# A written order for the start of a gated-mix kernel (FNet spectral branch and SwiGLU branch)

## The chip, the cores and the metric

The kernel runs on one core of one Trainium2 chip. The metric is the device time of one execution in microseconds (us); before the change the median of three runs is 711.37 us (711.16 to 711.52). A core has a matrix engine (TensorE, PE in the profile, whose weight loads have a row of their own, PEld), a vector engine (VectorE, DVE), an activation engine (ScalarE, ACT), GpSimd (POOL) and SyncE (SP). Each works through its own list of instructions in order; semaphores tie them together. DMAs are issued from SP, ACT or POOL.

## The reference, cut to what matters

```python
g = sigmoid((x * gate_w).sum(-1, keepdims=True))            # x: 2048 x 512
a = dft_seq_re @ (x @ dft_hid_re.T) - dft_seq_im @ (x @ dft_hid_im.T)
h = silu(x @ w1) * (x @ w3)                                 # w1, w3: 512 x 1376
b = h @ w2                                                  # w2: 1376 x 512
out = g * a + (1 - g) * b
```

All of it is float32. The change touches only the beginning of the work on `h`.

## The kernel before, in words

**Precision.** TensorE takes float32r operands. Each float32 block X is split into a high part (ScalarE copies X into a float32r tile: `high`, L108) and a low part (VectorE subtracts the high part from X: `low`, L111). A product of two blocks is then three matmuls, high·high, high·low and low·high, each 128 x 128 by 128 x 512.

**Fewer products.** 2 x 2 blocks of operands are multiplied with a seven-product scheme (Winograd's form of Strassen's), so sums of blocks are formed on VectorE first: on the x side T1 to T4 from the raw blocks B11, B12, B21, B22 (`sum_xo`, L207, and `split_xo`), on the weight side four sums of one weight set (`sums_wb`, L248 to L251), whose split parts are the tile `wb`. The three raw weight parts are the tile `wa`; of the four raw parts of a set, in the order of its load, the third is A22 and the fourth, A21, is needed raw only by the first item.

**Items.** The gate and up products run over `ITEMS`, pairs of a column chunk c of the weights and a half g of the tokens; one item gives two 128 x 512 blocks of `h`. An item has seven products of six matmuls. They go into PSUM banks: X (bank n % 4) takes four of them in turn, Y (bank 4 + n % 2) one, Z (bank 6 + n % 2) two. X and Y are begun LOOK = 3 items ahead: `first1(n)` is the first X product and its copy to `s1`, `first2(n)` the Y product, the addition `s1 += Y` on VectorE (L293), which frees the Y bank, and `gate1(n)` the Silu of `s1`. `gate_up(n)` does the rest of item n and, between its own products, `first1(n + 3)` and `first2(n + 3)`. Two lists, `early` and `mid`, hang further work into an item: `early` after its second bank of work is begun, `mid` after the low part of the next `wb`.

**The first items.** Item 0 is computed without the seven-product scheme (`plain`, eight half products of six matmuls into the banks C00, C10, C01, C11), because its operands arrive first. Then come `first1`, `first2` and `gate1` of items 1, 2 and 3, with all sums and splits that they and item 1 need written between them. A pool of warm-up matmuls (`WARM` = 11, L398) runs on a zeroed bfloat16 tile while the first loads are under way.

**Order.** Up to L674 (the line that switches to the written order, just before the loop over `gate_up`) the order of each engine's instructions is chosen by the scheduler from the program's dependencies; from there on every engine's list is the program order. The loads of the start all go through the SP queue: a 128 KB piece of weight set 0, x block B11 (512 KB), the other 384 KB of weight set 0, B21, B12, weight set 1, B22, weight sets 2 and 3.

Of the kernel before, what the change touches and what calls it, by code (L numbers as in the profile page):

```python
# [21 lines left out]
NG = NST // 2  # L22
NC = (F + P - 1) // P
NP2 = (NC + 1) // 2
WARM = 11
LOOK = 3
K = 9
W2_AT = (9, 11, 13, 15)
# [4 lines left out]
def fnet_swiglu_gate_kernel(  # L33
# [46 lines left out]
    def bank(k, name):  # L80
        return psum.tile([P, 512], F32, tag=f"ps{k}", name=name)
# [17 lines left out]
    def parts(name):  # L99
        return take(ZO, [P, 2, 4, 256], F32R, name)  # L100
# [12 lines left out]
    def split(hi, lo, src):  # L113
        high(hi, src)
        low(hi, lo, src)
# [79 lines left out]
    def load_xo(g, k):  # L195

        if g not in XO:
            XO[g] = (xo1 if g else xo0).tile([P, 2, 7, 2, 512], F32R, tag="xo", name=f"xo{g}")
        ST[g, k] = wide(f"xs{g}_{k}")
        nc.sync.dma_start(ST[g, k], xt[g, XRAW.index(k)])  # L200

    OPS = ("B11", "B21", "B22", "T1", "T2", "T3", "T4")
    SUMS = {"T1": ("B12", "B11"), "T2": ("B22", "T1"), "T3": ("B22", "B12"), "T4": ("B21", "T2")}
# [1 line left out]
    def sum_xo(g, k, t):  # L205
        ST[g, k] = t
        nc.vector.tensor_sub(t, *(ST[g, v] for v in SUMS[k]))  # L207
# [5 lines left out]
    def split_xo(g, k):  # L213
        split(*xo_parts(g, k))
# [6 lines left out]
    def load_w(w, lo=0, hi=4):  # L221
        if lo == 0:
            WS[w] = f4_a.tile([P, 4, 256], F32, tag=f"f4_{4 + w % (LOOK + 1)}", name=f"ws{w}")
        nc.sync.dma_start(WS[w][:, lo:hi].rearrange("p a n -> p (a n)"),  # L224
                          w13[SETS[w], :, lo * 256 : hi * 256])

    def load_wb(w, spare=False):
# [5 lines left out]
    def wa_parts(w, lo, hi):  # L233
        return (*(flat(WA[w][:, h, lo:hi]) for h in range(2)), flat(WS[w][:, lo:hi]))

    def prep_wa(w, lo=0, hi=3):

        if lo == 0:
            WA[w] = wap.tile([P, 2, 3, 256], F32R, tag="wa", name=f"wa{w}")
        split(*wa_parts(w, lo, hi))  # L240

    WU = {}

    def sums_wb(w):

        r = WS.pop(w)
        u = WU[w] = wup.tile([P, 4, 256], F32, tag="wu", name=f"wu{w}")
        nc.vector.tensor_add(u[:, 0], r[:, 3], r[:, 2])  # L248
        nc.vector.tensor_sub(u[:, 1], u[:, 0], r[:, 0])
        nc.vector.tensor_sub(u[:, 2], r[:, 0], r[:, 3])  # L250
        nc.vector.tensor_sub(u[:, 3], r[:, 1], u[:, 1])  # L251

    def wb_parts(w):
        return flat(WB[w][:, 0]), flat(WB[w][:, 1]), flat(WU[w])
# [1 line left out]
    def high_wb(w):  # L256
        WB[w] = wbp.tile([P, 2, 4, 256], F32R, tag="wb", name=f"wb{w}")
        high(wb_parts(w)[0], wb_parts(w)[2])

    def low_wb(w):  # L260
        low(*wb_parts(w))
        if w < K:
            nc.gpsimd.dma_start(wbsp[w], WB[w].bitcast(F32))

    def prep_wb(w):
        sums_wb(w)
        high_wb(w)
        low_wb(w)

    def prod(ps, n, wi, xi, start, chain=False):  # L270
        w = WSET[n]
# [15 lines left out]

    def first2(n):

        y = bank(4 + n % 2, f"Y{n}")  # L290
        prod(y, n, 1, 1, True)
        s1 = G[n][1]
        nc.vector.tensor_add(s1, s1, y)  # L293
        put_score(n, 0, s1)
# [37 lines left out]
    def gate_up(n):  # L332
        last = NI - 1
        x, s1 = G.pop(n)
        z = bank(6 + n % 2, f"Z{n}")
        if n == last - 1:

            u2, g1 = (s1p.tile([P, 512], F32, tag="s1", name=f"{k}_{n}") for k in ("u2", "g1"))
        else:
            h = hp.tile([P, 1024], F32, tag="h", name=f"h{n}")  # L340
            u2, g1 = h[:, :512], h[:, 512:]
        u4 = u4p.tile([P, 512], F32, tag="u4", name=f"u4_{n}")
        nw = WSET[n + 1] if n < last else 0
        if nw in WB or nw == 0:
            nw = None
        elif back(nw):
            load_wb(nw)
            nw = None
        wa = WSET[n + LOOK + 1] if n + LOOK < last else 0
        if wa in WA or wa == 0:  # L350
            wa = None
        else:
            load_w(wa, 0, 3 if back(wa) else 4)

        prod(x, n, 4, 4, False, True)
        nc.scalar.activation(u2, x, AF.Copy)
        run(early, n)
        prod(z, n, 5, 5, True, True)
        nc.scalar.activation(u4, z, AF.Copy)
        if nw is not None:  # L360
            sums_wb(nw)
        if n + LOOK <= last:
            first1(n + LOOK)
        if nw is not None:
            high_wb(nw)
        prod(x, n, 3, 3, False, True)
        nc.vector.tensor_add(u4, u4, x)  # L367
        if nw is not None:
            low_wb(nw)
        run(mid, n)  # L370
        prod(z, n, 2, 6, False, True)
        nc.vector.tensor_add(u2, u2, z)
        nc.vector.tensor_mul(u2, s1, u2)  # L373
        store_h(n, 0, u2)
        if wa is not None:
            WA[wa] = wap.tile([P, 2, 3, 256], F32R, tag="wa", name=f"wa{wa}")
            parts_a = wa_parts(wa, 0, 3)
            high(parts_a[0], parts_a[2])
        if n + LOOK <= last:
            first2(n + LOOK)  # L380
        if wa is not None:
            low(*parts_a)
        prod(x, n, 6, 2, False, True)
        nc.scalar.activation(g1, x, AF.Silu)
        put_score(n, 1, x)
        if n + LOOK <= last:
            gate1(n + LOOK)
        nc.vector.tensor_mul(g1, g1, u4)
        store_h(n, 1, g1)
        run(at_end, n)  # L390

    load_w(0, 0, 1)
    load_xo(0, "B11")
    warm = s1p.tile([P, 1024], mybir.dt.bfloat16, tag="s1", name="warm")[:, :512]
    nc.vector.memset(warm, 0.0)
    wps = bank(7, "wps")
    for n in range(WARM):
        nc.tensor.matmul(wps, warm[:, :P], warm, start=True, stop=True)  # L398
    nc.scalar.activation(act0, warm[:, :24], AF.Silu)

    def plain(b12, a21):

        c = {}

        def half(i, j, w, x, start):
            if start:
                c[i, j] = bank((0, 4, 6, 7)[2 * i + j], f"C{i}{j}")
            for r in range(2):
                sl = slice(r * P, (r + 1) * P)
                mm3(c[i, j], w(0, sl), w(1, sl), x(r, 0), x(r, 1), start and r == 0,  # L410
                    not start and r == 1)

        def wa(k):
            return lambda h, sl: WA[0][:, h, k, sl]

        def xb(k):
            return lambda q, h: XO[0][:, h, k, q, :]

        w21 = lambda h, sl: a21[:, h, sl]
        x12 = lambda q, h: b12[:, h, q * 512 : (q + 1) * 512]  # L420
        s1 = s1p.tile([P, 512], F32, tag="s1", name="s1_0")
        g1 = u4p.tile([P, 512], F32, tag="u4", name="g1_0")
        h = hp.tile([P, 1024], F32, tag="h", name="h0")
        yield half(0, 0, wa(0), xb(0), True)
        yield half(1, 0, w21, xb(0), True)
        half(0, 0, wa(1), xb(1), False)
        nc.scalar.activation(s1, c[0, 0], AF.Silu)
        yield half(1, 0, wa(2), xb(1), False)
        nc.vector.tensor_mul(h[:, :512], s1, c[1, 0])
        store_h(0, 0, h[:, :512])  # L430
        half(0, 1, wa(0), x12, True)
        yield half(1, 1, w21, x12, True)
        half(0, 1, wa(1), xb(2), False)
        nc.scalar.activation(g1, c[0, 1], AF.Silu)
        half(1, 1, wa(2), xb(2), False)
        nc.vector.tensor_mul(h[:, 512:], g1, c[1, 1])
        yield store_h(0, 1, h[:, 512:])

    load_w(0, 1, 4)
    load_xo(0, "B21")  # L440
    load_xo(0, "B12")
    load_w(1)
    load_xo(0, "B22")
    load_w(2)
    load_w(3)

    zt = parts("b12"), parts("a21")
    b12, a21 = zt[0].rearrange("p h a n -> p h (a n)"), zt[1][:, :, 0]
    step = plain(b12, a21)
    prep_wa(0, 0, 1)  # L450
    for q in range(2):
        split(XO[0][:, 0, 0, q], XO[0][:, 1, 0, q], ST[0, "B11"][:, q * 512 : (q + 1) * 512])
    next(step)
    split(a21[:, 0], a21[:, 1], WS[0][:, 3])
    next(step)
    prep_wa(0, 1, 3)
    split_xo(0, "B21")
    next(step)
    split(b12[:, 0], b12[:, 1], ST[0, "B12"])
    next(step)  # L460
    split_xo(0, "B22")
    next(step)
    free(*zt)
    WS.pop(0)
    load_w(4)
    prep_wa(1)
    first1(1)
    first2(1)
    gate1(1)
    sum_xo(0, "T1", hp.tile([P, 1024], F32, tag="h", name="t1"))  # L470
    sum_xo(0, "T2", ST[0, "B11"])
    prep_wa(2)
    first1(2)
    first2(2)
    gate1(2)
    split_xo(0, "T2")
    prep_wb(1)
    sum_xo(0, "T3", ST[0, "B12"])
    split_xo(0, "T3")
    prep_wa(3)  # L480
    first1(3)
    first2(3)
    gate1(3)
    split_xo(0, "T1")
    prep_wa(4)
    sum_xo(0, "T4", ST[0, "B21"])
    split_xo(0, "T4")
    free(*(ST[0, b] for b in ("B11", "B21", "B12", "B22")))

    def do(work, n, f, *a):  # L490
        work.setdefault(n, []).append(lambda: f(*a))


    for k in ("B11", "B21", "B12", "B22"):
# [176 lines left out]
        sum_c(m + LEAD + 1)  # L671
        split_c(m + LEAD)

    ctx.enter_context(tc.manual_schedule())  # L674
    for n in range(1, NI):
        gate_up(n)
        if ITEMS[n] == (NC - 1, 0):
# [317 lines left out]
```

## Time and profile before

| What | Value |
|---|---|
| median of 3 runs | 711.37 us (711.16 to 711.52) |
| the profiled execution: its time | 710.88 us |
| the profiled execution: its span, first to last instruction | 709.1 us |
| PE busy | 703.9 us, 3089 matmuls |
| VectorE busy | 604.6 us, 733 instructions |
| ScalarE busy | 369.6 us, 478 instructions |
| DMA | 172.54 MB, mean 243 GB/s |

Times in the profile are counted from the span's start. A row of the timeline gives the start, the length, the engine, the line, the operation with its output and inputs, the count, and in brackets how long the engine stood idle before it and what released it. Tile names have their numbers left out, so that all PSUM tiles X1, X2, ... read X. A "xo" is a split x block, "xs_B" a raw one, "ws" raw weights, "wu" sums of weights.

### The profile page before, as it was taken

Reading aid. Unit: us, or ns where it says so; the run is one execution under the profiler, and the core shown is the slowest. Engines: PE = TensorE matmul, PEld = TensorE weight load, DVE = VectorE, ACT = ScalarE, POOL = GpSimd, SP = SyncE. Lnnn points to the kernel's source line nnn. Section 1 sums busy time; section 2 is a strip of 40 time slices with the busy share of each in tenths; the row PEclk is TensorE's granted clock in tenths of the full one; section 3 lists DMA queues with packets and bytes.
Section 4 is the critical chain, followed back from the end, with each engine's and each line's share of the span. In section 5 each row is a group of like instructions: output and inputs, shape, how many; then the busy total and the mean of one; then the engine's idle time right before and its main releaser. Section 6 shows DMA issues by size and latency. Waiting matters only on the chain.

```text
span 709.1 us, 8589 instructions
## 1 busy us (share of the span) xinstructions
PE 703.9 (99%) x3089; PEld 579.1 (82%) x3089; DVE 604.6 (85%) x733; ACT 369.6 (52%) x478; POOL 64.0 (9%) x118
## 2 busy tenths in 40 slices
PE   9999999999999999999999999999999999999997
PEld 6888888888888888888888888888888888888886
DVE  6979988787679999887999599969997896898985
ACT  6665555655446754454554553544455455455451
POOL 0011111121110000000110001100110000000000
PEclk9999999999999999999999999999999999999999
DMA  7575546589997556712596238814999971773932
GB/s 281 196 295 215 211 188 253 186 313 359 413 412 271 220 207 232 288 60 89 175 358 254 90 122 322 342 48 190 382 419 416 354 270 58 296 285 135 323 119 89
DMA packets 45403, 172.54 MB, mean 243 GB/s; under 512 B 5296, under 2 KB 5424, under 8 KB 41520
## 3 DMA queue, kind: packets, MB, share of 16 engines
q1 hardware_dynamic: 32464, 118.50, 45.2%
q0 software_dynamic: 12608, 52.97, 18.9%
q8 instruction: 24, 0.39, 0.2%
q10 hardware_dynamic: 288, 0.52, 0.2%
q14 instruction: 19, 0.16, 0.1%
HBM read 114.82 MB, written 57.16 MB: 243 GB/s over the span
## 4 chain that ended last, share of the span: by engine, by line
PE 99%; DMA 1%; DVE 0%; ACT 0%; SPq 0%; issue 0%
PE P L119 69%; PE X L119 16%; PE Z L119 8%; PE Y L119 4%; PE C L119 2%; DMA xs_B<-xt 1%; DVE xo L111 0%; DVE zc L788 0%; ACT xo L108 0%; SPq L224 0%
## 5 line engine op out<-in xcount | busy, mean ns | idle before, releaser
L119 PE MATMUL P<-zo,a 128*128 128x512 f32 x1344 | 305.5, 390 | 0.0
L119 PEld LDWEIGHTS P<-zo,a 128*128 128x128 f32 x1344 | 252.1, 188 | 53.2 <-DVE zo L111 1.2
L108 ACT ACTIVATE zo<-B 128x1024 fp32r<-128x1024 f32 (+1 forms) x182 | 189.3, 1045 | 184.5 <-PE P L119 93.2
L111 DVE TENSOR_TENSOR zo<-B,zo 128x1024 fp32r<-128x1024 f32 (+1 forms) x182 | 217.9, 1204 | 48.2 <-ACT zo L108 47.4
L119 PE MATMUL P<-zo,H 128*128 128x512 f32 x468 | 106.2, 389 | 0.0
L119 PEld LDWEIGHTS P<-zo,H 128*128 128x128 f32 x468 | 87.9, 188 | 18.2
L645 DVE TENSOR_TENSOR B<-B,B 128x1024 f32<-128x1024 f32 (+1 forms) x78 | 93.0, 1192 | 0.1
L119 PE MATMUL X<-xo,wb 128*128 128x512 f32 x378 | 92.7, 390 | 0.0
L119 PEld LDWEIGHTS X<-xo,wb 128*128 128x128 f32 x378 | 71.0, 188 | 14.7
L119 PE MATMUL P<-zo,Y 128*128 128x512 f32 x336 | 76.3, 390 | 0.0
L119 PEld LDWEIGHTS P<-zo,Y 128*128 128x128 f32 x336 | 63.1, 188 | 13.1
L322 POOL DMA_DIRECT2D hsp<-h x42 | 23.0, 547 | 126.5 <-DVE h L373 75.6
L119 PE MATMUL X<-xo,wa 128*128 128x512 f32 x126 | 32.3, 390 | 0.0
L119 PE MATMUL Z<-xo,wa 128*128 128x512 f32 x126 | 32.3, 391 | 0.0
L119 PE MATMUL Y<-xo,wa 128*128 128x512 f32 x126 | 32.1, 390 | 0.0
L119 PE MATMUL Z<-xo,wb 128*128 128x512 f32 x126 | 32.1, 390 | 0.0
L648 DVE TENSOR_TENSOR B<-B,B 128x1024 f32<-128x1024 f32 x26 | 31.7, 1219 | 0.0
L863 ACT ACTIVATE zu<-P 128x512 f32<-128x512 f32 x32 | 19.1, 598 | 20.4 <-PE P L119 20.3
L367 DVE TENSOR_TENSOR u<-u,X 128x512 f32<-128x512 f32 x21 | 14.4, 687 | 17.7 <-PE X L119 15.5
L119 PEld LDWEIGHTS Z<-xo,wa 128*128 128x128 f32 x126 | 23.6, 188 | 5.3 <-DVE xo L111 0.4
L119 PEld LDWEIGHTS Y<-xo,wa 128*128 128x128 f32 x126 | 23.7, 188 | 4.9
L119 PEld LDWEIGHTS X<-xo,wa 128*128 128x128 f32 x126 | 23.7, 188 | 4.9
(134 smaller groups left out, 551.3 us busy)
## 6 DMA issues: line engine op xcount, KB each, us to landing
B<-cc SPq DMA_DIRECT2D x64, 512.0 KB, 6.1
hsp<-h POOLq DMA_DIRECT2D x42, 256.0 KB, 3.6
B<-hsp SPq DMA_DIRECT2D x20, 512.0 KB, 9.9
wbsp<-wb POOLq DMA_DIRECT2D x8, 1024.0 KB, 4.3
wb<-wbsp SPq DMA_DIRECT2D x8, 1024.0 KB, 7.8
B<-zsp SPq DMA_DIRECT2D x16, 512.0 KB, 8.4
H<-w2sp SPq DMA_DIRECT2D x6, 1024.0 KB, 9.0
ws<-w SPq DMA_DIRECT2D x11, 512.0 KB, 6.1
```

The lines of the kernel that those rows point to most:

```text
L108: nc.scalar.activation(hi, src, AF.Copy)
L111: nc.vector.tensor_sub(lo, src, hi.bitcast(F32))
L119: nc.tensor.matmul(ps, u, v, start=first and n == 0, stop=last and n == 2, skip_group_check=chain)
L322: nc.gpsimd.dma_start(hsp[g, b + k, j // 2, :, j % 2 * 512 : (j % 2 + 1) * 512], h)
L367: nc.vector.tensor_add(u4, u4, x)
L645: nc.vector.tensor_add(t, t, RAW[blk, b, q][:, :n])
L648: nc.vector.tensor_sub(t, RAW[blk, "B12", q], t)
L863: nc.scalar.activation(U[name][:, r], ps[r], AF.Copy)
```

## The change

Everything up to the loop over the items now has a written order too. In the pieces:

- the switch to the written order is put ahead of the first load, and the generator `plain` becomes a straight sequence of `half` calls with the other work between them;
- B11 of the first half of x is loaded as two DMAs of 256 KB; the 384 KB of weight set 0 go through the ACT queue;
- warm-up runs on the program's constant 1.0 with 10 matmuls instead of 11, and VectorE's memset goes away;
- the six matmuls of a half product of item 0 are put in the order high·high, low·high for both row blocks, then the two high·low (before: all three of one row block, then of the other);
- `first2` is cut into `prod2` (the product) and `sum_g` (the addition that frees the Y bank). For item 1 the addition and the Silu follow soon; for item 2 they are put into `mid` of item 1, for item 3 into `early` of item 2;
- of weight sets 2, 3 and 4 only the first two parts are split at the start; the third part, A22, used by an item's second Z product, is split in `mid` of items 1, 2 and 3;
- high part of T4, the first two sums of weight set 2 and the low part of T4 are put into `early` of item 1.

```diff
-        nc.sync.dma_start(ST[g, k], xt[g, XRAW.index(k)])
+        n = 512 if not g and k == "B11" else 1024
+        for i in range(0, 1024, n):
+            nc.sync.dma_start(ST[g, k][:, i : i + n], xt[g, XRAW.index(k), :, i : i + n])
...
-        nc.sync.dma_start(WS[w][:, lo:hi].rearrange("p a n -> p (a n)"),
+        (nc.scalar if lo else nc.sync).dma_start(WS[w][:, lo:hi].rearrange("p a n -> p (a n)"),
...
     def first2(n):
 
+        sum_g(n, prod2(n))
+
+    def prod2(n):
         y = bank(4 + n % 2, f"Y{n}")
         prod(y, n, 1, 1, True)
+        return y
+
+    def sum_g(n, y):
         s1 = G[n][1]
         nc.vector.tensor_add(s1, s1, y)
...
-            sums_wb(nw)
+            sums_wb(nw, 2 if nw in WU else 0)
...
+    ctx.enter_context(tc.manual_schedule())
...
-    warm = s1p.tile([P, 1024], mybir.dt.bfloat16, tag="s1", name="warm")[:, :512]
-    nc.vector.memset(warm, 0.0)
+    warm = nc.const_aps.tensor(1.0, [P, 512], mybir.dt.bfloat16)
...
+        v = ([(wp(h, sl), xp(r, 0)) for sl, r in v for h in range(2)]
+             + [(wp(0, sl), xp(r, 1)) for sl, r in v])
...
+    half(0, 0, 1, 1, False)
+    split(b12[:, 0], b12[:, 1], ST[0, "B12"])
+    nc.scalar.activation(s1, C[0, 0], AF.Silu)
+    half(1, 0, 2, 1, False)
+    new_wa(1)
+    sums_wb(1, 0, 1)
+    split(*wa_parts(1, 0, 3))
...
+    first1(1)
+    y1 = prod2(1)
+    sums_wb(1, 2, 4)
+    high_wb(1)
+    sum_g(1, y1)
+    gate1(1)
+    sum_xo(0, "T3", ST[0, "B12"])
+    low(*wa_parts(3, 0, 2))
+    first1(2)
+    y2 = prod2(2)
+    high(*xo_parts(0, "T3")[::2])
+    low_wb(1)
+    low(*xo_parts(0, "T3"))
+    first1(3)
+    y3 = prod2(3)
+    new_wa(4)
+    split(*wa_parts(4, 0, 2))
+    low(*xo_parts(0, "T1"))
+    sum_xo(0, "T4", ST[0, "B21"])
...
+    do(early, 1, lambda: high(*xo_parts(0, "T4")[::2]))
+    do(early, 1, sums_wb, 2, 0, 2)
+    do(early, 1, lambda: low(*xo_parts(0, "T4")))
+    do(early, 1, free, *(ST[0, b] for b in ("B11", "B21", "B12", "B22")))
+    for n, work, at, y in ((2, mid, 1, y2), (3, early, 2, y3)):
+        do(work, at, sum_g, n, y)
+        do(work, at, gate1, n)
+    for w in (2, 3, 4):
+        do(mid, w - 1, lambda v=wa_parts(w, 2, 3): split(*v))
```

More of the change, by code (lines that the diff above doesn't have):

```diff
@@ L24 @@
 NP2 = (NC + 1) // 2
-WARM = 11
+WARM = 10
 LOOK = 3
@@ L234, in wa_parts, with new_wa, sums_wb @@
         return (*(flat(WA[w][:, h, lo:hi]) for h in range(2)), flat(WS[w][:, lo:hi]))
[L236 to L240, printed above, removed]
+    def new_wa(w):
+        WA[w] = wap.tile([P, 2, 3, 256], F32R, tag="wa", name=f"wa{w}")
     WU = {}
[L244 to L251, printed above, removed]
+    def sums_wb(w, lo=0, hi=4):
+        r = WS[w]
+        if w not in WU:
+            WU[w] = wup.tile([P, 4, 256], F32, tag="wu", name=f"wu{w}")
+        u = WU[w]
+        for i, (f, a, b) in enumerate(((nc.vector.tensor_add, r[:, 3], r[:, 2]),
+                                       (nc.vector.tensor_sub, u[:, 0], r[:, 0]),
+                                       (nc.vector.tensor_sub, r[:, 0], r[:, 3]),
+                                       (nc.vector.tensor_sub, r[:, 1], u[:, 1]))):
+            if lo <= i < hi:
+                f(u[:, i], a, b)
     def wb_parts(w):
@@ L263, in low_wb @@
             nc.gpsimd.dma_start(wbsp[w], WB[w].bitcast(F32))
[L265 to L268, printed above, removed]
     def prod(ps, n, wi, xi, start, chain=False):
@@ L375, in gate_up @@
         if wa is not None:
-            WA[wa] = wap.tile([P, 2, 3, 256], F32R, tag="wa", name=f"wa{wa}")
+            new_wa(wa)
             parts_a = wa_parts(wa, 0, 3)
@@ L399, in fnet_swiglu_gate_kernel @@
     nc.scalar.activation(act0, warm[:, :24], AF.Silu)
[L401 to L437, printed above, removed]
     load_w(0, 1, 4)
-    load_xo(0, "B21")
-    load_xo(0, "B12")
+    for k in ("B21", "B12"):
+        load_xo(0, k)
     load_w(1)
@@ L448, in fnet_swiglu_gate_kernel, with half @@
     b12, a21 = zt[0].rearrange("p h a n -> p h (a n)"), zt[1][:, :, 0]
-    step = plain(b12, a21)
-    prep_wa(0, 0, 1)
+    C = {(i, j): bank((0, 4, 6, 7)[2 * i + j], f"C{i}{j}") for i in range(2) for j in range(2)}
+    new_wa(0)
+    def half(i, j, w, x, start):
+        v = [(slice(r * P, (r + 1) * P), r) for r in range(2)]
+        wp = lambda h, sl: a21[:, h, sl] if w is None else WA[0][:, h, w, sl]
+        xp = lambda q, h: b12[:, h, q * 512 : (q + 1) * 512] if x is None else XO[0][:, h, x, q, :]
+        v = ([(wp(h, sl), xp(r, 0)) for sl, r in v for h in range(2)]
+             + [(wp(0, sl), xp(r, 1)) for sl, r in v])
+        for n, (a, b) in enumerate(v):
+            nc.tensor.matmul(C[i, j], a, b, start=start and n == 0,
+                             stop=not start and n == len(v) - 1)
+    s1 = s1p.tile([P, 512], F32, tag="s1", name="s1_0")
+    g1 = u4p.tile([P, 512], F32, tag="u4", name="g1_0")
+    h0 = hp.tile([P, 1024], F32, tag="h", name="h0")
+    t1 = hp.tile([P, 1024], F32, tag="h", name="t1")
+    split(*wa_parts(0, 0, 1))
     for q in range(2):
         split(XO[0][:, 0, 0, q], XO[0][:, 1, 0, q], ST[0, "B11"][:, q * 512 : (q + 1) * 512])
-    next(step)
+    half(0, 0, 0, 0, True)
     split(a21[:, 0], a21[:, 1], WS[0][:, 3])
-    next(step)
-    prep_wa(0, 1, 3)
+    half(1, 0, None, 0, True)
+    split(*wa_parts(0, 1, 3))
     split_xo(0, "B21")
-    next(step)
+    half(0, 0, 1, 1, False)
     split(b12[:, 0], b12[:, 1], ST[0, "B12"])
-    next(step)
-    split_xo(0, "B22")
-    next(step)
+    nc.scalar.activation(s1, C[0, 0], AF.Silu)
[3 more added lines that the diff above has]
+    split(*wa_parts(1, 0, 3))
+    nc.vector.tensor_mul(h0[:, :512], s1, C[1, 0])
+    store_h(0, 0, h0[:, :512])
+    half(0, 1, 0, None, True)
+    split_xo(0, "B22")
+    half(1, 1, None, None, True)
+    sum_xo(0, "T1", t1)
+    new_wa(2)
+    high(*wa_parts(2, 0, 2)[::2])
+    half(0, 1, 1, 2, False)
+    nc.scalar.activation(g1, C[0, 1], AF.Silu)
+    sum_xo(0, "T2", ST[0, "B11"])
+    low(*wa_parts(2, 0, 2))
+    half(1, 1, 2, 2, False)
     free(*zt)
@@ L465, in fnet_swiglu_gate_kernel @@
     load_w(4)
-    prep_wa(1)
+    sums_wb(1, 1, 2)
+    split_xo(0, "T2")
+    high(*xo_parts(0, "T1")[::2])
+    nc.vector.tensor_mul(h0[:, 512:], g1, C[1, 1])
+    store_h(0, 1, h0[:, 512:])
+    new_wa(3)
+    high(*wa_parts(3, 0, 2)[::2])
     first1(1)
-    first2(1)
+    y1 = prod2(1)
+    sums_wb(1, 2, 4)
+    high_wb(1)
+    sum_g(1, y1)
     gate1(1)
-    sum_xo(0, "T1", hp.tile([P, 1024], F32, tag="h", name="t1"))
-    sum_xo(0, "T2", ST[0, "B11"])
-    prep_wa(2)
+    sum_xo(0, "T3", ST[0, "B12"])
+    low(*wa_parts(3, 0, 2))
     first1(2)
[L474 to L480, printed above, removed]
+    y2 = prod2(2)
+    high(*xo_parts(0, "T3")[::2])
+    low_wb(1)
+    low(*xo_parts(0, "T3"))
     first1(3)
[L482 to L485, printed above, removed]
+    y3 = prod2(3)
+    new_wa(4)
+    split(*wa_parts(4, 0, 2))
+    low(*xo_parts(0, "T1"))
     sum_xo(0, "T4", ST[0, "B21"])
-    split_xo(0, "T4")
-    free(*(ST[0, b] for b in ("B11", "B21", "B12", "B22")))
     def do(work, n, f, *a):
         work.setdefault(n, []).append(lambda: f(*a))
+    do(early, 1, lambda: high(*xo_parts(0, "T4")[::2]))
[7 more added lines that the diff above has]
+        do(mid, w - 1, lambda v=wa_parts(w, 2, 3): split(*v))
     for k in ("B11", "B21", "B12", "B22"):
@@ L672, in advance @@
         split_c(m + LEAD)
-    ctx.enter_context(tc.manual_schedule())
     for n in range(1, NI):
```

## The prediction, made before the changed kernel was run

> **What bounds the kernel now.** I read the page first: its head, the busy times, and the chain that ended last.
>
> ```profile
> span 709.1 us, 8589 instructions
> PE 703.9 (99%) x3089; PEld 579.1 (82%) x3089; DVE 604.6 (85%) x733; ACT 369.6 (52%) x478; POOL 64.0 (9%) x118
> PE 99%; DMA 1%; DVE 0%; ACT 0%; SPq 0%; issue 0%
> ```
>
> TensorE carries the end. A change at the start matters only by when TensorE gets through the same matmuls. So the second view is the list of waits of its weight loads, which shows stalls that the overlapping matmul records hide (total us, times, longest).
>
> ```profile
> PEld P L119 <- DVE zo L111: 1.2, 4, 0.4
> PEld C L119 <- DVE xo L111: 0.9, 2, 0.5
> PEld C L119 <- ACT xo L108: 0.5, 1, 0.5
> PEld Z L119 <- DVE xo L111: 0.4, 1, 0.4
> ```
>
> The P waits lie behind the changed region; the other 1.8 us lie in it. The third view is the chain in order of time.
>
> ```profile
> 31.41 1.43 PE Z L119 x5
> 32.83 1.36 PE Y L119 x6
> ...
> 217.79 487.58 PE P L119 x2148
> ```
>
> Six matmuls take 1.36 us, 0.227 each (487.58 / 2148 = 0.227 too), and from 31.41 on they follow without a break to the last block. Any time by which TensorE is early or late at the Y product of 32 us is therefore passed to the end. That product, the Y of item 4, is my measuring point: the matmuls ahead of it are the same in number in both kernels.
>
> The start, from the timeline:
>
> ```profile
> 0.32 0.10 POOL L985 MEMSET const-bfloat16-1.0<- 128x1 bf16 x1
> 0.73 1.28 ACT L399 ACT_TABLE_LOAD   x1 [0.73 <-PEq L985]
> 0.74 0.39 SPq L224 DMA_DIRECT2D ws<-w  x1
> 1.19 4.67 PE L398 MATMUL wps<-warm 128*128 128x512 bf16 x11 [1.19 <-DVE warm L395]
> 3.21 0.42 ACT L108 ACTIVATE wa<-ws 128x256 fp32r<-128x256 f32 x1 [0.96 <-DMA ws<-w]
> 4.94 1.15 ACT L108 ACTIVATE xo<-xs_B 128x512 fp32r<-128x512 f32 x2 [1.31 <-DMA xs_B<-xt]
> 5.62 0.19 PEld L119 LDWEIGHTS C<-xo,wa 128*128 128x128 f32 x1 [0.46 <-ACT xo L108]
> 6.00 0.40 ACT L108 ACTIVATE a<-ws 128x256 fp32r<-128x256 f32 x1
> 6.30 0.62 ACT L108 ACTIVATE wa<-ws 128x512 fp32r<-128x512 f32 x1
> 7.19 1.06 ACT L108 ACTIVATE xo<-xs_B 128x1024 fp32r<-128x1024 f32 x1 [0.27 <-DMA xs_B<-xt]
> 8.29 1.23 DVE L111 TENSOR_TENSOR xo<-xs_B,xo 128x1024 fp32r<-128x1024 f32 x1 [0.45 <-ACT xo L108]
> 8.46 1.06 ACT L108 ACTIVATE b<-xs_B 128x1024 fp32r<-128x1024 f32 x1 [0.21 <-DMA xs_B<-xt]
> 9.57 2.14 PEld L119 LDWEIGHTS C<-xo,wa 128*128 128x128 f32 x10 [0.40 <-DVE xo L111]
> 11.74 1.32 PEld L119 LDWEIGHTS C<-b,wa 128*128 128x128 f32 x6
> ```
>
> A block arrives, ScalarE makes its high part, VectorE its low part, TensorE follows. The first matmul waits for B11 (landed at 4.92), the ten at 9.57 for the low part of B21.
>
> **Part 1, the first 24 matmuls.** Warm-up on a constant: VectorE's memset no longer holds TensorE to 1.19. The constant is there by 0.42, ScalarE and SP start at 0.73 and 0.74, so I estimate a start near 0.75; ten matmuls at 4.67 / 11 = 0.425 end near 5.0. B11 in halves: B21 and B12, 512 KB each, landed 1.27 apart (7.17 and 8.44, by the ends of ScalarE's waits), so 256 KB is 0.64 and the first half lands near 4.3 (bounds: 3.2, when the 128 KB piece landed, and 4.92). The first real matmul comes at about 5.0 instead of 5.62. That gain does not last: matmuls 17 on need B21's low part, and as many bytes as before lie ahead of B21, so I leave its landing at 7.17, the low part at 9.52, TensorE at 9.57. What changes is how many matmuls stand behind that point. With the high-part matmuls first, and the order of the two C products as written, four run ahead of it and eight behind; before, two and ten. Matmul 25 comes at 9.57 + 8 x 0.227 = 11.38 against 11.74: **0.36 us gained**.
>
> The weights on the ACT queue (384 KB): the table load and one small activation stand ahead of that DMA. Bounds: it lands at 5.86 as before, or, if all of B21 passes it, at 7.17. ScalarE splits these weights before B21 and would then start B21's split about 0.8 later (0.30 and 0.5 for its two weight splits, by the starts at 6.00 and 6.30 and the 0.62 of the second). I take equal sharing of the DMA engines, by which the weights land by 6.2 and B21's split still starts at 7.19.
>
> **Part 2, between 11.4 and 32.** There are 90 matmuls to item 4's Y in both kernels. Before they took 20.70 (11.74 to 32.44, below), 90 x 0.227 = 20.4 and one stall for T4's low part. Laying the new order of VectorE against its durations I find about 0.2 waited for the low part of weight set 3 and none for T4. TensorE would reach item 4's Y at 11.38 + 20.4 + 0.2 = 32.0 instead of 32.44.
>
> **Part 3, the wait that the change adds.** Item 4's Y goes into the bank of item 2's Y, which is free once VectorE has added that Y to `s1`. Before, this was early:
>
> ```profile
> 19.54 0.42 DVE L251 TENSOR_TENSOR wu<-ws,wu 128x256 f32<-128x256 f32 x1
> 23.88 0.68 DVE L293 TENSOR_TENSOR s<-s,Y 128x512 f32<-128x512 f32 x1
> 24.47 0.95 DVE L111 TENSOR_TENSOR wa<-ws,wa 128x768 fp32r<-128x768 f32 x1
> 27.35 1.22 DVE L207 TENSOR_TENSOR xs_B<-xs_B,xs_B 128x1024 f32<-128x1024 f32 x1
> 29.08 0.42 DVE L248 TENSOR_TENSOR wu<-ws 128x256 f32<-128x256 f32 x1
> 30.12 1.23 DVE L111 TENSOR_TENSOR xo<-xs_B,xo 128x1024 fp32r<-128x1024 f32 x1 [0.17 <-ACT xo L108]
> 31.60 0.42 DVE L251 TENSOR_TENSOR wu<-ws,wu 128x256 f32<-128x256 f32 x1
> 31.94 0.68 DVE L367 TENSOR_TENSOR u<-u,X 128x512 f32<-128x512 f32 x1
> 32.05 1.06 ACT L108 ACTIVATE wb<-wu 128x1024 fp32r<-128x1024 f32 x1 [0.96 <-DVE wu L251]
> 32.44 1.33 PEld L119 LDWEIGHTS Y<-xo,wa 128*128 128x128 f32 x6
> 33.15 1.23 DVE L111 TENSOR_TENSOR wb<-wu,wb 128x1024 fp32r<-128x1024 f32 x1 [0.53 <-ACT wb L108]
> 34.29 0.68 DVE L372 TENSOR_TENSOR h<-h,Z 128x512 f32<-128x512 f32 x1
> 18.00:24.00 6.00, 6.00 (x9) 1.00 0.40 134
> 24.00:30.00 6.00, 5.92 (x8) 1.00 0.49 192
> ```
>
> The last two rows are VectorE's busy time in two windows of 6 us: it is full there. The addition ended at 24.56, TensorE needed the bank at 32.44. The change puts the addition into `mid` of item 1, on VectorE's list right behind the low part of `wb` 2: the place that `h += Z` had at 34.29. VectorE takes its list in order, and that low part waits for ScalarE, which waits for the last sum of set 2. On TensorE only Z's six matmuls, 1.36 us, stand between the X product that `u += X` reads and this Y.
>
> When does VectorE get there? Steps between starts of its dense rows are 1.14 for a 1.22 row, 0.87 for 0.95, 0.60 for 0.68, 0.34 for 0.42 (0.45 where it reads the one before).
> - Last sum of set 1: 19.54 before. ScalarE now takes the Silu of C00 (ready at about 10.4, half a us) ahead of weight set 1, so that split runs late and VectorE's low part starts at 11.8 instead of 11.04. With a shorter set 2 (-0.27), a wait for T2's high part (+0.27), a dependent T1 to T2 step (+0.12) and an old wait gone (-0.34), the sum starts at 20.1.
> - From there to the first sum of set 2 it was 9.54 (19.54 to 29.08). Two additions go (-1.19), two splits shrink from 768 to 512 columns (-0.54), a wait for weight set 4's high part comes (+0.34): 8.15, so 28.25.
> - T4's high part on ScalarE from 28.4, 1.06 long; low part on VectorE at 29.5; the last two sums at 30.6 and 31.0; `wb` high at 31.4 to 32.5; `wb` low at 32.5; the addition at 33.65, ended at 34.3; TensorE at 34.4.
>
> TensorE then waits from 32.0 to 34.4, 2.4 us, and starts that Y **1.96 us later** than before. The matmuls behind it find their operands ready: item 5's weights, the next late ones (VectorE's 256-column rest of set 2 has to wait for ScalarE, which puts the Silu of item 2 first), are done near 38.6, their third matmul's turn is 40.3. Without the Y wait they would cost 0.6. Items 2 and 3 get 0.34 more on VectorE each, covered, as a rising Y and X chain leaves it some 2 us there. `s1 += Y` of item 3 is needed for item 5's Y at 43.9 and comes near 39.1.
>
> Bounds of the 1.96: even with everything else ready, `u += X` (0.60), `wb` low (1.14) and the addition (0.68) follow the X product, 2.4 with hand-overs and the last matmul's 0.39 near 2.9, of which Z hides 1.36: at least 1.5 waited, +1.0 net. Above, VectorE no earlier than before: 34.29 + 0.68 + 0.06 = 35.0, +2.6; with late weights of part 1, +3.2.
>
> **Sum.** On the profiled execution (710.88, its span 709.1 and 1.8 around it) this gives 712.84; on the median, 711.37 + 1.96 = **713.3**. 0.2% is 1.42 us, about what a measurement of this kernel can tell from no change.
>
> **Rivals.**
> - *The bank is free in time.* If VectorE and ScalarE are 2.4 us earlier at that point, the addition ends by 32.0 and only part 2's 0.4 remains: 711.0, not slower. It decides from the point at which the addition ends ahead of 32.0. For it: two additions and 512 columns taken off VectorE ahead of it. Against: VectorE is full from 18 to 30, and the X product alone forces 1.5. A wait cut to under 1.8 ends within 0.2% too. Chance 0.17.
> - *The matmul rate falls in the gap.* Before, TensorE worked from 1.19 to about 5.4 at 0.425 a matmul and then at 0.227. If 2.4 idle us brought the slow rate back for as long, 4.2 us, 4.2 x (1 - 0.227 / 0.425) = 2.0 more are lost: 715.3. Against: the longest stall before, by the list of waits, was 0.5, so no row shows it. Chance 0.05. The Trainium skill, "TensorE: Matmul & The Clock Gate", section "Part 1: The HAM clock gate", has the rate drop only after an idle window of some 3.4 us; by that rule 2.4 us leave it fast and the sum stands.
> - *The weights on the ACT queue land last.* Then B21's split starts 0.8 late and VectorE carries it to item 4's Y: 714.1. For it: that DMA is issued behind a 1.3 us table load. Chance 0.07, inside the range.
>
> My forecast has 0.71. **How the numbers follow:** the likeliest time is 713.3. The range goes from +0.9 to +3.2 on the median, 712.2 to 714.6, with both bounds of part 3 and the late weights. Slower by over 0.2%: forecast 0.71 less a tenth of it below 1.42, and the two slower rivals, 0.76. Faster by over 0.2% needs the bank free and more gained ahead than I find: 0.02. Within: 0.22.
>
> **What would show it.** A PEld wait of Y on DVE `s` of some 2.4 us near 32 to 34, and nothing like it for the next Y; the eight C loads from 9.57; matmul 25 near 11.4; no Z wait. I am wrong if Y has no wait, if matmuls behind it are spaced 0.425, or if B21's split starts later than 7.3.

## The result and the profile after

The changed kernel takes 714.91 us (median of 6 runs, 713.67 to 715.34) beside 711.43 us (711.16 to 711.68) of the kernel before on the same chip: ratio 1.0045, 95% interval 1.0032 to 1.0058, so it is slower by about 0.45%. That is 1.6 us above the forecast of 713.3 and 0.3 above the end of the range. The six runs fall into two groups: 713.67 and 713.70, with a mean granted clock (the share of TensorE's full speed that the profile reports) of 1.000 and 0.999, and four from 714.74 to 715.34, with 0.997 or 0.998. The profiled execution is one of the lower two: 713.70, its span 711.9 (before: 710.88 and 709.1).

The list of waits of the weight loads after (total us, times, longest) has a new wait of Y, and the first C products wait longer for x (the line of the warm-up's own matmuls is left out):

```profile
...
PEld C L430 <- ACT xo L108: 2.7, 3, 2.0
PEld Y L119 <- DVE s L298: 2.4, 1, 2.4
PEld P L119 <- DVE zo L111: 1.1, 4, 0.4
PEld C L430 <- DVE xo L111: 0.7, 2, 0.5
PEld X L119 <- DVE wa L111: 0.2, 1, 0.2
```

The start after, from the timeline (start, length, engine and group, in brackets the idle time before it and who ended it):

```profile
0.74 1.28 ACT L406 ACT_TABLE_LOAD   x1 [0.74 <-PEq L1000]
0.78 4.12 PE L405 MATMUL wps<-const-bfloat16-1.0 128*128 128x512 bf16 x10 [0.78 <-PEq L1000]
0.80 0.38 ACTq L226 DMA_DIRECT2D ws<-w  x1
4.07 0.42 ACT L108 ACTIVATE wa<-ws 128x256 fp32r<-128x256 f32 x1 [1.82 <-DMA ws<-w]
5.60 1.32 ACT L108 ACTIVATE xo<-xs_B 128x512 fp32r<-128x512 f32 x2 [1.11 <-DMA xs_B<-xt]
6.28 0.30 PEld L430 LDWEIGHTS C<-xo,wa 128*128 128x128 f32 x2 [1.99 <-ACT xo L108]
8.36 1.06 ACT L108 ACTIVATE xo<-xs_B 128x1024 fp32r<-128x1024 f32 x1 [0.61 <-DMA xs_B<-xt]
10.73 1.69 PEld L430 LDWEIGHTS C<-xo,wa 128*128 128x128 f32 x8 [0.49 <-DVE xo L111]
11.50 0.60 ACT L447 ACTIVATE s<-C 128x512 f32<-128x512 f32 x1 [0.82 <-PE C L430]
12.46 1.32 PEld L430 LDWEIGHTS C<-b,wa 128*128 128x128 f32 x6
```

The warm-up and the eight loads behind B21's low part are there as forecast, but every block of x is late: the first half of B11 is split at 5.60 (the whole block at 4.94 before), B21 at 8.36 (7.19 before). Matmul 25 starts at 12.46, 0.72 later than before.

The stretch at item 4's Y after, from the timeline:

```profile
32.25 0.68 DVE L372 TENSOR_TENSOR u<-u,X 128x512 f32<-128x512 f32 x1
32.37 1.06 ACT L108 ACTIVATE wb<-wu 128x1024 fp32r<-128x1024 f32 x1 [0.99 <-DVE wu L255]
33.46 1.23 DVE L111 TENSOR_TENSOR wb<-wu,wb 128x1024 fp32r<-128x1024 f32 x1 [0.53 <-ACT wb L108]
34.60 0.68 DVE L298 TENSOR_TENSOR s<-s,Y 128x512 f32<-128x512 f32 x1
35.34 1.23 PEld L119 LDWEIGHTS Y<-xo,wa 128*128 128x128 f32 x6 [2.42 <-DVE s L298]
35.34 1.66 PE L119 MATMUL Y<-xo,wa 128*128 128x512 f32 x6 [2.00 <-DVE s L298]
...
44.79 1.32 PEld L119 LDWEIGHTS Y<-xo,wa 128*128 128x128 f32 x6
```

`s1 += Y` of item 2 stands behind the low part of `wb` 2, and item 4's Y waits 2.42 us for it (its matmuls stand idle for 2.00). It starts at 35.34 against 32.44 before: 2.90 later, and the span is 2.8 longer. From there to item 5's Y are 9.45 us, 42 matmuls at 0.225, without a break. So in this execution the whole loss lies ahead of 35.4. The last wait in that list is the one that I expected of weight set 3; no Z waits.

### The profile page after: what moved, and what is told of

Same layout as the page of the kernel before. It is cut to its first block, busy times and chain, and to the rows that moved or that the text cites. A ratio compares the mean times of both kernels' runs of the same rounds, so it can differ in the third digit from the quotient of the medians.

```text
span 711.9 us, 8590 instructions
## 1 busy us (share of the span) xinstructions
PE 704.0 (99%) x3088; PEld 578.3 (81%) x3088; DVE 604.8 (85%) x735; ACT 369.5 (52%) x481; POOL 64.2 (9%) x118
## 4 chain that ended last, share of the span: by engine, by line
PE 97%; DVE 1%; DMA 1%; ACT 1%; SPq 0%; issue 0%; ACTq 0%
PE P L119 68%; PE X L119 15%; PE Z L119 8%; PE Y L119 4%; PE C L430 1%; DMA xs_B<-xt 1%; DVE xo L111 1%; ACT xo L108 0%; DVE wb L111 0%; DVE xs_B L209 0%; ACT wb L108 0%; SPq L202 0%; DVE zc L803 0%; DVE wa L111 0%; DVE wu L255 0%
```

## The experiments

Three questions: is the wait of Y the loss? Which of the two load edits makes x late? And what lifts four of six runs by another 1 us and more? Every kernel was timed beside the kernel before on the same chip: e1 to e4 on one chip, e5 to e8 on a second, e9 to e11 on a third, where the medians of the kernel before are 711.46, 711.39 and 711.22. Where a diff is given it is against the changed kernel.

**e1: the changed kernel again, unchanged.**

> The changed kernel as it is, to see its runs beside those of its variants. It has given 713.7 in two runs and 714.7 to 715.3 in four. If the four are runs in which TensorE works for some 4 us at the slow matmul rate, a profile of one such run (if it falls so) shows matmuls spaced 0.425 us somewhere after the start, and the mean granted clock of those runs is again 0.997 to 0.998 against 0.999 to 1.000. If instead a DMA is late in them, the spacing stays 0.227 and the list of waits shows more than the 2.4 us of Y, 2.7 and 0.7 of C.

Measured: 715.45 (714.51 to 715.91, 5 runs), ratio 1.005 (1.0038 to 1.0062); all five runs at a mean clock of 0.997 or 0.998. This time the profile caught an execution of the upper group (715.83, span 714.1). From its timeline, item 4's Y and item 5's Y:

```profile
35.91 1.49 PEld L119 LDWEIGHTS Y<-xo,wa 128*128 128x128 f32 x6 [2.43 <-DVE s L298]
35.91 2.21 PE L119 MATMUL Y<-xo,wa 128*128 128x512 f32 x6 [2.01 <-DVE s L298]
46.97 1.32 PEld L119 LDWEIGHTS Y<-xo,wa 128*128 128x128 f32 x6
```

The same 42 matmuls take 11.06 us in place of 9.45: 1.6 more. Single matmuls among them start at 37.49, 37.92, 38.35, 38.77 and 39.20, 0.43 apart in place of 0.227. The windows of TensorE show why (window, length, busy time and count, granted clock, DMA share, GB/s); first e1:

```profile
30.00:35.00 5.00, 3.90 (x18) 1.00 0.67 221
35.00:40.00 5.00, 4.09 (x11) 0.68 1.02 418
40.00:45.00 5.00, 5.00 (x23) 0.98 0.54 205
```

and the changed kernel's first profile:

```profile
35.00:40.00 5.00, 4.66 (x20) 1.00 1.01 410
```

Soon behind the wait the granted clock falls: 5 x 0.32 + 5 x 0.02 = 1.7 us of full-rate work is missing. The rival of the lost matmul rate has happened here.

These 1.6 us are not the whole difference of 2.1 us between the two profiled executions. Item 4's Y comes 0.57 later in e1, though B21 landed no later than in the first profile (8.1 against 8.3). That part lies at the start of e1, whose matmul 25 comes at 13.01 and not at 12.46:

```profile
6.09 2.93 PE L430 MATMUL C<-xo,wa 128*128 128x512 f32 x6 [0.89 <-ACT xo L108]
5.00:10.00 5.00, 4.11 (x11) 1.00 1.02 390
```

The matmuls at 6.69, 7.11, 7.54, 7.97, 8.39 and 8.82 are again 0.43 apart: the slow rate, which the warm-up had to its end in e1, is there behind the gap as well. The clock column does not tell it; it reads 1.00 in this window, as it does in the window of the warm-up, 0 to 5 us. So a run can be lifted in two ways: by a slow stretch that lowers its mean clock, and by a slow start that does not.

**e2: item 2's addition moved forward, from `mid` to `early` of item 1** (behind the low part of T4, ahead of `u += X` and `wb`). Nothing else changes.

```diff
-    for n, work, at, y in ((2, mid, 1, y2), (3, early, 2, y3)):
-        do(work, at, sum_g, n, y)
-        do(work, at, gate1, n)
+    do(early, 1, sum_g, 2, y2)
+    do(mid, 1, gate1, 2)
+    do(early, 2, sum_g, 3, y3)
+    do(early, 2, gate1, 3)
```

> The changed kernel with one move: item 2's addition of Y goes from the place behind the low part of the second weight sums to the place behind T4's low part, ahead of the last two weight sums. Theory (the held bank costs 2.4 us): the Y wait falls from 2.4 to under 0.2 us, nothing takes its place, and the time falls by 2.4 from the same level: 711.3 (from 713.7), or 712.5 (from 714.9). If the slow runs come of the 2.4 us gap, they are gone too. Rival (the wait is only the sign of a VectorE that is late with everything): another wait of 1 us or more appears at item 1's Z or item 5's X and the time stays above 712.8.

Measured: 711.37 (710.82 to 712.72, 11 runs), ratio 0.9999 (0.999 to 1.0008). The wait of Y is gone from the list of waits of e2:

```profile
PEld C L430 <- ACT xo L108: 2.5, 2, 2.2
...
PEld P L119 <- DVE zo L111: 1.1, 4, 0.4
PEld X L119 <- DVE wa L111: 0.2, 1, 0.2
```

One VectorE instruction in another place brings the median back to that of the kernel before, 3.5 us below the changed kernel's. Between the lower groups it is 2.7 us (713.7 to about 711.0; 2.4 was expected), and the rest is that four of six runs lay in the upper group there and five of eleven do here. The upper group is not gone, as it would be if the gap at Y alone made it: six runs lie from 710.82 to 711.37, five from 712.05 to 712.72. The profile is of the upper five, and its granted clock falls too, but at the start, behind the wait of the first C product, 2.2 us by the weight loads and 1.70 by the matmuls. From the timeline of e2:

```profile
6.08 2.65 PE L430 MATMUL C<-xo,wa 128*128 128x512 f32 x6 [1.70 <-ACT xo L108]
```

and from its windows of TensorE:

```profile
5.00:10.00 5.00, 3.92 (x10) 0.68 0.99 388
```

Of the five, only 712.05 and 712.54 have a mean clock of 0.997; the other three have 0.999, so a fall of the granted clock does not account for them. A slow start as in e1 would fit, but no profile shows one of the three.

**e3: weights on SP's queue again, B11 still in halves.**

```diff
-        (nc.scalar if lo else nc.sync).dma_start(WS[w]...
+        nc.sync.dma_start(WS[w]...
```

> The changed kernel with the 384 KB of weight set 0 back on the SP queue, behind the two halves of B11. Theory (the ACT queue's load was issued at 0.80, ahead of x, and takes the DMA engines from it): the 128 KB piece lands near 3.2 instead of 4.05, the first half of B11 near 4.3 instead of 5.6, B21 near 7.2 instead of 8.34, the Y wait stays 2.4, and the time falls by 0.8 to 1.1. Rival (the halves, of 2 KB rows, move slowly): the 128 KB piece comes earlier, but B21 still lands at 8 or later and the time falls by less than 0.3.

Measured: 714.75 (713.54 to 716.38, 6 runs), ratio 1.0046 (1.0032 to 1.006). ScalarE's rows of e3, each at the landing of a load:

```profile
3.19 0.42 ACT L108 ACTIVATE wa<-ws 128x256 fp32r<-128x256 f32 x1 [0.94 <-DMA ws<-w]
5.07 1.29 ACT L108 ACTIVATE xo<-xs_B 128x512 fp32r<-128x512 f32 x2 [1.46 <-DMA xs_B<-xt]
8.31 1.06 ACT L108 ACTIVATE xo<-xs_B 128x1024 fp32r<-128x1024 f32 x1 [0.67 <-DMA xs_B<-xt]
```

The 128 KB piece is early again (3.19, not 4.07), the first half comes 0.5 earlier, yet B21 is as late as ever. The queue alone is not why B21 is late.

**e4: B11 whole again, weights still on the ACT queue.**

```diff
-        n = 512 if not g and k == "B11" else 1024
+        n = 1024
```

> The changed kernel with B11 loaded as one DMA of 512 KB; the weights stay on the ACT queue. Theory (the ACT queue is to blame): the 128 KB piece still lands near 4, B11 near 5.9, B21 near 8, time within 0.4 of the changed kernel's. Rival (the rows of 2 KB are to blame): B21 lands near 7.2 and the time falls by about 1.0.

Measured: 716.24 (714.67 to 716.39, 6 runs), ratio 1.0059 (1.0047 to 1.007), the slowest of all. ScalarE's rows of e4:

```profile
4.24 0.42 ACT L108 ACTIVATE wa<-ws 128x256 fp32r<-128x256 f32 x1 [1.99 <-DMA ws<-w]
6.26 1.15 ACT L108 ACTIVATE xo<-xs_B 128x512 fp32r<-128x512 f32 x2 [1.61 <-DMA xs_B<-xt]
8.15 1.04 ACT L108 ACTIVATE xo<-xs_B 128x1024 fp32r<-128x1024 f32 x1
```

Neither forecast came out: the time rose by 1.3. With the weights on the second queue the 128 KB piece is 1.0 late and B11 1.3 (4.94 before), and the first C product waits up to 2.6 us; four of the six runs have mean clocks of 0.994 to 0.997. B21's split at 8.15 is held by ScalarE itself, which is busy with B11 and the weights until then, and does not tell when B21 landed. The DMA's issue and its time to landing do: 1.66 + 5.9 = 7.6, where the changed kernel has 2.13 + 6.2 = 8.3, e3 2.60 + 5.7 = 8.3 and the kernel before 2.12 + 5.0 = 7.1. So with B11 whole most of B21's delay is gone, as the rival said; its split stays late because B11 is late.

**e5: both load edits undone.** The diffs of e3 and e4 together.

> The changed kernel with the first load as before: the 384 KB of weight set 0 on the SP queue and B11 as one DMA. Theory (both the 2 KB rows and the ACT queue delay the loads; each was undone alone and B21 stayed late): B21 lands at 7.2 as before instead of 8.3, the first matmul comes at 5.6, matmul 25 near 11.4, the Y wait stays 2.4, item 4's Y starts near 34.3 instead of 35.3. Runs without a slow stretch near 712.7, with one near 714.3. Rival (the warm-up constant or the written order of the queue delays B21): B21 lands after 8 and nothing moves.

Measured: 714.57 (712.88 to 716.23, 6 runs), ratio 1.0046 (1.0035 to 1.0058). From the timeline of e5:

```profile
5.01 1.15 ACT L108 ACTIVATE xo<-xs_B 128x512 fp32r<-128x512 f32 x2 [1.43 <-DMA xs_B<-xt]
7.59 1.06 ACT L108 ACTIVATE xo<-xs_B 128x1024 fp32r<-128x1024 f32 x1 [0.36 <-DMA xs_B<-xt]
34.57 2.21 PEld L119 LDWEIGHTS Y<-xo,wa 128*128 128x128 f32 x6 [2.43 <-DVE s L298]
```

B11 is at 5.01, no later than its first half in e3, and B21 0.7 earlier than there: the halves gain nothing and delay what follows. B21 landed at 7.6 as in e4, so it is the halves and not the queue that B21 pays for. It is still split 0.4 behind the kernel before (7.2 was expected); nothing here shows why. From the windows of all engines (the last two columns are DMA share and GB/s), e3:

```profile
4.00:6.00 2.00, 1.05 (x4) 0.40 (x3) 0.34 (x2) 0.91 (x2) 0.00 (x0) 1.00 0.97 322
```

and e5:

```profile
4.00:6.00 2.00, 0.93 (x4) 0.40 (x3) 0.36 (x2) 0.99 (x2) 0.00 (x0) 1.00 1.01 394
```

The DMA engines are as full in both, but 322 GB/s are moved with the halves and their rows of 2 KB, and 394 with the whole block and its rows of 4 KB. In the same window the five profiles with B11 whole (before, e4, e5, e6, e9) have 358 to 423 GB/s, the eight with halves 240 to 345. Whether the shorter rows do it or the additional DMA was not separated. Item 4's Y starts at 34.57, 0.8 earlier than in the changed kernel and 0.2 from the forecast's 34.4, and its wait is the same 2.43. The best run, 712.88, is 0.4 under the forecast; the other five, 714.33 and up, have clocks of 0.997 and 0.998.

**e6: e2 and e5 together**, the addition early and both load edits undone.

> Both undone: the first load as before and item 2's addition of Y ahead of the last two weight sums. Theory: no Y wait, matmul 25 near 11.4 against 11.74 before, and from there a steady stream; the idle time after the warm-up is 0.7 us, too short for a slow stretch. 710.5 to 711.0, 0.4 to 0.9 below the kernel before, in nearly all runs. Rival (the gain of the new order of matmuls is lost elsewhere): 711.4 or more with another wait in the list.

Measured: 710.78 (710.29 to 712.26, 11 runs), ratio 0.9992 (0.9984 to 1.0001), on the edge of what can be told from no change. Its profile has no wait of Y, and item 4's Y at

```profile
32.39 1.32 PEld L119 LDWEIGHTS Y<-xo,wa 128*128 128x128 f32 x6
```

where the kernel before has 32.44. B21 was split at 7.79 in it, so matmul 25 came at 11.89 and not near 11.4. Two of the eleven runs, 712.0 and 712.26, still lie apart.

**e7: both gaps filled.** Four more warm-up matmuls, and eleven matmuls on the constant ahead of item 4's Y, into a bank of their own; nobody reads their results. The wait of Y itself stays.

```diff
-WARM = 10
+WARM = 14
...
+        if n == 1:
+            fps = bank(6, "fps")
+            for i in range(11):
+                nc.tensor.matmul(fps, warm[:, :P], warm, start=True, stop=True)
```

> The changed kernel with TensorE kept busy in its two gaps: 14 warm-up matmuls instead of 10, and 11 matmuls on the constant into a free bank ahead of item 4's Y. The added matmuls compute nothing that is used. Theory (the runs above 714 are those in which the idle gap brings the slow matmul rate back): Y still starts at about 35.4, the granted clock is 1.00 in every window after 7 us, the mean clock is 0.999 to 1.000 in all runs, and all runs lie within 0.5 of 713.8; median 1.1 to 1.6 below the changed kernel's. Rival (the slow runs are chance or a DMA): the runs spread up to 715 or more as without it.

Measured: 713.53 (713.26 to 713.94, 7 runs), ratio 1.0029 (1.0018 to 1.004). All runs have clocks of 0.999 or 1.000 and lie within 0.7 us. The weight loads of e7 in the gap and behind it:

```profile
33.40 2.08 PEld L387 LDWEIGHTS <-const-bfloat16-1.0 128*128 128x128 bf16 x11 [0.26 <-issue]
35.61 1.33 PEld L119 LDWEIGHTS Y<-xo,wa 128*128 128x128 f32 x6
```

and TensorE's window behind it:

```profile
35.00:40.00 5.00, 5.00 (x24) 1.00 1.01 394
```

VectorE's addition still holds the bank, until 35.53, and Y starts no earlier than in the changed kernel (35.61 against 35.34), and yet the median is 1.4 lower. Idleness of TensorE, not the lateness of Y, makes the upper group.

**e8: e2 with WARM 14**, to fill the gap at the start where it was the only one left.

> The kernel with the bank freed early (late loads as in the change) with 14 warm-up matmuls instead of 10, which reach from 0.8 to about 6, up to the first real matmul. Theory (a slow stretch after the gap of some 2 us at the start made the runs of 712.0 to 712.7): these disappear, all runs lie at 710.8 to 711.4. Rival (too many warm-up matmuls push the start): first matmul after 6.5 and all runs above 711.4.

Measured: 711.07 (710.84 to 711.56, 11 runs), ratio 0.9995 (0.9987 to 1.0004). The upper group of e2 is gone: none of eleven runs is above 711.6, where five of eleven were above 712. TensorE's window of e8 (e2 has 0.68 there):

```profile
5.00:10.00 5.00, 4.90 (x20) 1.00 0.98 389
```

**e9: e6 with WARM 12**, all of it together.

> The kernel with the bank freed early and the first load as before, with 12 warm-up matmuls instead of 10: they reach from 0.8 to about 5.9, to the first real matmul. Theory: the few runs of 712.0 to 712.3 without it came of the 0.7 to 1.3 us gap at the start and are gone; all runs at 710.2 to 711.0, median 710.5, 0.9 below the kernel before. Rival (the last warm-up matmuls delay the start by what they save): median 710.9 or more.

Measured: 710.59 (710.39 to 711.05, 11 runs) beside 711.22 (710.89 to 711.96, 22 runs): ratio 0.999, 0.9981 to 0.9999. It beats both kernels, by 0.6 us of the kernel before. From the weight loads of e9:

```profile
11.50 1.32 PEld L430 LDWEIGHTS C<-b,wa 128*128 128x128 f32 x6
31.99 1.32 PEld L119 LDWEIGHTS Y<-xo,wa 128*128 128x128 f32 x6
```

Here is what part 1 and part 2 of the prediction looked for: matmul 25 at 11.50 (forecast 11.38), item 4's Y at 31.99 (32.0).

**e10: the changed kernel with WARM 14 alone**, to see how much of its upper group the gap at the start makes.

> The changed kernel with 14 warm-up matmuls and nothing in the gap at item 4's Y. It tells which of the two gaps brings the slow stretch in the changed kernel. Theory (the 2.4 us at Y does): runs still spread, some at 715 or above with the granted clock below 1.00 in the window 35 to 40 us, median 714.3 or more. Rival (the gap at the start does): all runs at 713.3 to 714.0 as with both gaps filled.

Measured: 713.43 (713.0 to 715.08, 6 runs), ratio 1.0035 (1.0023 to 1.0046): four runs from 713.0 to 713.51 with clocks of 0.999 and 1.000, two at 715.0 and 715.08 with 0.997 and 0.998. I had expected a median of 714.3, because I put the upper group down to the gap at Y almost alone. That was too much: with the gap at Y only, two of six runs fall into it, with both gaps nine of eleven (the four of six above and the five of e1). Both take part; with so few runs the shares are rough.

**e11: the kernel before with the two load edits alone.**

> The kernel before with the two edits of the load alone: B11 in halves, 384 KB of weight set 0 on the ACT queue. Theory (they delay the loads): the 128 KB piece lands after 3.6 instead of 3.2, B21 near 8.0 to 8.3 instead of 7.17, matmul 25 starts near 12.7 instead of 11.74, and the time rises by 0.7 to 1.2 us, 712.1 to 712.6. Rival (earlier first half helps): the first matmul comes before 5.6 and the time is 711.4 or less.

Measured: 711.86 (711.52 to 713.12, 11 runs) beside 711.22: ratio 1.001 (1.0001 to 1.0019), 0.64 us, a little less than the 0.7 to 1.2 expected. From the timeline of e11:

```profile
4.20 0.42 ACT L108 ACTIVATE wa<-ws 128x256 fp32r<-128x256 f32 x1 [1.52 <-DMA ws<-w]
8.32 1.06 ACT L108 ACTIVATE xo<-xs_B 128x1024 fp32r<-128x1024 f32 x1 [0.53 <-DMA xs_B<-xt]
33.61 1.34 PEld L119 LDWEIGHTS Y<-xo,wa 128*128 128x128 f32 x6
```

The late B21 (8.32) comes with the loads, whatever the order of the other work. In this profile item 4's Y is 1.17 late; the median shows half of that.

## Why the prediction was right or wrong

- **The wait of Y: right.** Forecast 2.4 us on VectorE's `s`, measured 2.42 here, 2.43 in e1, e3, e4 and e5; e2 removes it and with it the loss. The steps between VectorE's rows that I counted (`u += X`, `wb`, the addition) are there: the addition starts at 34.60 where I had 33.65, and all of that difference is there at the start already, as the next point shows. TensorE was ready for this Y at 32.9 where I had 32.0, late by as much, so the length of the wait came out while both of its ends did not. The rival that the bank comes free in time (0.17) fell.
- **B21's landing: the smaller of the two steps that failed.** I wrote that "as many bytes as before lie ahead of B21, so I leave its landing at 7.17". Equal bytes did not take equal time. B21 was split at 8.36, the low part followed at 9.45, and the term of -0.36 at matmul 25 became +0.72. VectorE carried it on through the Silu of C00 (11.50, forecast 10.4) to item 4's Y: 35.34 instead of 34.4. With both load edits undone (e5) it is 34.57. The half block that I expected at 4.3 came at 5.60: I had scaled it by its bytes, but e3 shows the first half no earlier than the whole block in e5. "B21's split starts later than 7.3" was one of my signs of being wrong.
- **The rival on the ACT queue: wrong in its reason.** I gave 714.1 if the weights landed last, with B21's split 0.8 late, since their DMA would be issued behind the table load. B21's split came 1.17 late, but not for that: the DMA was issued at 0.80, while that load ran (0.74 to 2.02), and landed 3.8 later, at 4.6, ahead of both my bounds (5.86 and 7.17). The two load edits cost different things. The queue delays the 128 KB piece and B11: 4.2 and 6.3 in e4 against 3.2 and 5.0 in e5. The halves delay B21: by issue and landing it came at 7.7 to 8.4 in the eight profiles that have them, at 7.4 to 7.8 in the four of the new order that do not. These are single executions, and one of the eight (e10, 7.7) lies among the four. My upper end also took 2.6 and these 0.8 as 3.2; they make 3.4, 714.8, which the median exceeds as well.
- **The lost matmul rate: the step that failed and took the median out of the range.** My sum put it at nothing and left it to a rival of 0.05; it sets the median. The two runs that keep the rate, 713.7, are 2.25 above before, in place of 1.96, inside the range; the four others add 1.0 to 1.6. e1's profile shows the mechanism, e7 and e8 remove it by filling the gaps alone. I argued that no row showed it, since the longest stall before was 0.5. That gave no bound at all for a wait more than four times as long, and the 2.0 us that I had worked out for the loss (measured 1.6) belonged with a much larger chance. With it the likeliest time would have been near 715. I also counted only the gap at Y; that the late x makes a second one, 1.99 by the weight loads, follows from the failed step above. Matmuls spaced 0.425 behind Y were another of my signs of being wrong, and e1 has them. Either step alone stays in the range, if only just: 713.7 in the two runs that keep the rate, 714.57 in e5, where x is 0.4 late at most.
- **The rule that I let stand.** By the Trainium skill, "TensorE: Matmul & The Clock Gate", section "Part 1: The HAM clock gate", the rate drops after an idle window of some 3.4 us, and I let that rule stand for the 2.4 us here. The traces of this case differ: 2.01 us idle at Y (e1) and 1.70 at the start (e2) were enough, in part of the executions. The measurement decides.
- **The sum.** 711.43 + 1.96 (wait of Y, less the start's gains) + about 0.3 (late loads: 0.9 in item 4's Y of the profile, less by the times of the two runs that keep the rate, since the profiled execution of the kernel before, 710.88, lies 0.55 under its median) = 713.7, and with the lost rate of 1.0 to 1.6 in four of six runs the median of 714.91.

What stays open: why one execution of the same kernel loses the rate and the next does not. The kernel before has such runs too, if rarely: of its 64 runs beside e1 to e11 three lie above 713, one with a mean clock of 0.997, and none of them has a profile. No profile shows what TensorE's clock goes by.

## What to carry to other kernels

An addition that reads a PSUM bank and is put off holds the bank: ask who writes into it next, and put the addition ahead of that, not merely ahead of whoever needs its sum. A gap of some 2 us in TensorE cost more than its length here, in part of the executions; where it can't be removed, matmuls on a constant in it cost no time that could be seen (e7) and kept the rate. A small load on a second queue, or a block cut in two, was not free for the loads beside it: the block that the critical chain waits for (here B21) must be looked at, not the one that was moved.

## What the runs showed of the hardware that I had not expected

- The slow stretch that the clock column shows is equally long in all four profiles that have one (e1, e2, e4, e5). If the rate in it is half (0.43 a matmul in e1 against 0.227), the granted clocks give its length: 2 x (5 x 0.32 + 5 x 0.02) = 3.4 us in e1. In e4 it lies across two windows at the start:

```profile
5.00:10.00 5.00, 3.25 (x11) 0.85 1.03 419
10.00:15.00 5.00, 5.00 (x19) 0.81 0.85 338
```

2 x (5 x 0.15 + 5 x 0.19) = 3.4 us again. In these profiles an idle 1.7 to 2.0 us is followed by a slow 3.4 us. That is the length of the window that the Trainium skill names in "TensorE: Matmul & The Clock Gate", section "Part 1: The HAM clock gate".
- The granted clock of the profile reads 1.00 while the warm-up's matmuls are 0.43 apart (the eleven in e7's gap, on the same constant, 0.2), and still 1.00 where that rate goes on behind the gap (e1, 5 to 10 us). A slow start is seen in the spacing of the matmuls, not in the clock.
- The DMA engines, equally full, moved 322 GB/s with one block cut into two DMAs of 2 KB rows and 394 without (e3, e5; the window of 4 to 6 us).
- A DMA on ScalarE's queue goes out at 0.80, while ScalarE's table load of 1.28 us runs from 0.74.
